# Preparing three more head pairs with VectorE transposes, and taking the mask constant from exp's bias

## The chip, the cores and the metric

The kernel runs on one core of a Trainium2 chip. The metric is the time of one execution in microseconds (us), measured on the device; a lower number is better. Before the change the median was 326.76 us of three runs (325.74 to 328.09). Repeated runs of one kernel spread by 1 to 1.5%, so a difference of 0.3% between two single runs says nothing. A run more than 1.5% above the fastest of its kernel counts as slow and is left out of the ratios. "The profile" and "the trace" are records of one profiled execution of each kernel. Its span is about 2 us shorter than the device time.

## The reference, cut to what matters

There are 4 batches of 8 heads, 768 positions, 64 dimensions a head, and 16 cluster centroids a head. A query sees only the keys of its own cluster. The result goes through a hidden layer with sin.

```python
q_assign = argmax(einsum('bhsd,hcd->bhsc', q_n, c_n), -1)     # k_assign likewise
mask     = q_assign[:, :, :, None] == k_assign[:, :, None, :]
scores   = where(mask, q @ k.T / sqrt(D), -1e9)
attn     = exp(scores - max(scores)); attn = attn / (sum(attn) + 1e-9)
x        = attn @ v                                           # heads side by side, 512 wide
h        = x @ w_in;  g = h + sin(alpha * h)**2 / (alpha + 1e-9)
out      = g @ w_out
```

## The kernel before

Heads are handled two at a time. There are 16 such pairs, m = 0 to 15, four in a batch. A pair takes 12 steps, so a batch takes 48. One step multiplies one block of scores into one of two buffers of PSUM (`scores`), takes its exp (`expo`, 128x768), and multiplies an older exp with v (`pv`). After each batch comes a hidden stage (w_in, sin, w_out), whose rest fills the steps of the next batch.

The mask is put into the matmul. Each query and key carries, besides its 64 dimensions, 16 rows that are 1 in the row of its cluster, and one row more, the sign row: +1 for queries, -1 for keys. The product of these 17 rows is 0 where the clusters agree and -1 where they don't. The exp's scale is 32, so a masked score is multiplied by exp(-32).

```python
KR = D + NHC + 1                       # 64 + 16 + the sign row
NPE = 2 * NHP                          # pairs 0 to 7 are prepared by TensorE
trp = ctx.enter_context(tc.tile_pool(name="trp", bufs=2))
...
def expo(i):
    pT = ptp.tile([P, S], BF16, tag="pT", name="pT")
    nc.scalar.activation(out=pT, in_=area(i)[:, 0:S], func=ACTF.Exp, scale=escale)
```

Before a pair's scores can start, its q and k are loaded (`load_qk`), transposed so that the 64 dimensions lie on partitions (tile `T32`), copied into the bf16 operand tile `QK` by GpSimd (`prep_cast`), multiplied with the centroids (`prep_asn`, the cluster product), turned into one-hot rows in four pieces by VectorE (`prep_hot`), and these rows are moved into `QK` by four small DMAs (`prep_move`). There are two ways of transposing:

```python
def prep_T(m, g, bk=None, eng="dve"):  # TensorE: three fp32 transposes, then one copy
    for jj in range(NJ2):
        nc.tensor.transpose(out=bk[:, P*jj : P*jj+P], in_=src[:, h, P*jj : P*jj+P], identity=ident_f)
    nc.vector.tensor_scalar_mul(out=s["T32"][:, g, :], in0=bk[:, 0:HS], scalar1=1.0 / QDIV)
...
def prep_D(m, g):                      # VectorE: 32x32 blocks are transposed in place ...
    nc.vector.transpose(out=s["Tq"][:, g, :], in_=src[:, h, :].rearrange("p (j e d) -> p e j d", e=2, d=32))
def prep_S(m):                         # ... and 8 DMAs carry the blocks to their partitions
    s["T32"] = trp.tile([P, 4, HS], F32, tag="T32", name="T32")
    for i in range(4):
        for e in range(2):
            lo = D * (i // 2) + 32 * e
            nc.sync.dma_start(out=s["T32"][lo : lo+32, :, ...], in_=s["Tq"][32*i : 32*i+32, :, ...])
...
first = {1: 0, 2: 4, 3: 12, 4: 20, 5: 28, 6: 36}     # the step at which a pair's preparation starts
# prep(m, s0), for m >= NPE: prep_D at s0-5.., prep_S at s0-2; then s0 += 12;
# prep_cast at s0+2 and s0+4; prep_asn at s0+5: 19 steps from the DMAs to their reader
...
# w_in and w_out: four loads at steps 23, 30, 36, 42 of batch 0, four at step 47
```

The way by VectorE spares TensorE, but it puts DMAs between the load and the cluster product, and these need time to land. The kernel before uses it from pair 8 on.

The softmax here doesn't subtract the row's maximum and nothing guards it: scores larger than these inputs give would overflow.

## Time and profile before

| stage (us) | before |
|---|---|
| head: start to first exp | 14.09 |
| batch 0: first exp to the first sin table | 44.43 |
| hidden stage 0 | 29.85 |
| batch 1, 2, 3 | 43.47, 43.75, 41.57 |
| hidden stages 1, 2 | 29.68, 29.45 |
| tail: from the last sin table | 48.71 |
| span | 325.0 |

The stages are cut at ScalarE's table loads: a stage of attention is the time from an exp table to the next sin table. In the page of the profile of before, the lines below are: busy time of each engine, the clock that TensorE was granted and the DMA engines' busy share (each digit is tenths, in one of 40 slices), the share of each engine in the chain that ended last, two groups of instructions (busy time, mean ns of one, idle time before them), and one group of DMAs (KB each, us from issue to landing).

```profile
span 325.0 us, 7163 instructions
PE 306.9 (94%) x2744; PEld 183.3 (56%) x2787; DVE 206.1 (63%) x361; ACT 241.7 (74%) x325; POOL 112.6 (35%) x175
...
PEclk9989999999999999999999999999999999999999
DMA  7455398993016959550043858520043200000031
...
PE 70%; ACT 10%; DVE 9%; issue 5%; POOL 3%; DMA 2%; SPq 1%; ACTq 0%; DVEq 0%; POOLq 0%
...
L319 ACT ACTIVATE pT<-S 128x768 bf16<-128x768 f32 x192 | 145.3, 810 | 27.1 <-PE S L314 24.8
...
L400 ACT ACTIVATE s_sb<-S,alpha_col 128x768 bf16<-128x768 f32 x44 | 39.4, 902 | 24.2 <-PE S L389 14.2
...
T<-Tq SPq DMA_DIRECT2D x64, 96.0 KB, 3.4
```

TensorE is busy for 94% of the span, its clock is full nearly everywhere, and DMA is 2% of the chain. Two groups of ScalarE deserve a second look: the exp and the sin have the same shape and the same source in PSUM, but the exp, with immediate scale, takes 810 ns, and the sin, whose scale is a tile of one value a partition (`alpha_col`), takes 902 ns.

The next view is the table of windows for batch 0 (busy us of each engine with its count, then the clock, the DMA engines' busy share, and GB/s).

```profile
core 0: us, PE busy (x) PEld busy (x) DVE busy (x) ACT busy (x) POOL busy (x), PEclk, DMA share, GB/s
14.00:62.00 48.00, 45.20 (x537) 30.50 (x536) 35.22 (x67) 38.40 (x49) 37.46 (x49) 0.96 0.69 171
...
19.50:58.30 38.80, 36.05 (x452) 24.84 (x452) 30.67 (x59) 32.72 (x43) 31.66 (x41) 1.00 0.66 168
```

From 19.5 to 58.3 TensorE is busy 36.05 of 38.80 us and ScalarE 32.72. The timeline of ScalarE: its columns are start, duration, engine, line, operation, count of instructions in a row without a gap, and in brackets the idle time before, with its releaser.

```profile
14.09 1.51 ACT L319 ACTIVATE pT<-S 128x768 bf16<-128x768 f32 x2 [3.03 <-PE S L314]
...
46.48 4.70 ACT L319 ACTIVATE pT<-S 128x768 bf16<-128x768 f32 x6 [0.64 <-PE S L314]
...
261.52 9.16 ACT L319 ACTIVATE pT<-S 128x768 bf16<-128x768 f32 x12 [0.25 <-PE S L314]
```

Every gap shown is ended by a score matmul of TensorE.

### The profile page before, as it was taken

The numbers are of one execution on the slowest core, as the hardware profiler recorded it, in microseconds if no ns is written. First come the engines' busy times: TensorE is split into PE (matmuls) and PEld (weight loads), VectorE is DVE, ScalarE is ACT, GpSimd is POOL, SyncE is SP. The second block draws the span as 40 slices with busy tenths as digits, with TensorE's granted clock in tenths as the row PEclk, the third lists the DMA queues.
The fourth block names the chain that finished last, engine by engine and source line by source line (L and its number), as shares of the span: only waits on it lengthen the run. The fifth ranks groups of instructions, "written<-read, shape, count | busy, mean of one in ns | idle before, by whom it ended". The sixth has DMA issues, their size and how long they took to land.

```text
span 325.0 us, 7163 instructions
## 1 busy us (share of the span) xinstructions
PE 306.9 (94%) x2744; PEld 183.3 (56%) x2787; DVE 206.1 (63%) x361; ACT 241.7 (74%) x325; POOL 112.6 (35%) x175
## 2 busy tenths in 40 slices
PE   6699999899999999999999999999999999999995
PEld 3276666555555665555556565555556566555544
DVE  4468888387837566677837766677836522577721
ACT  5388888787778988787678888787778999687300
POOL 7848797620017089530005476430006200000000
PEclk9989999999999999999999999999999999999999
DMA  7455398993016959550043858520043200000031
GB/s 228 139 189 162 123 217 187 216 206 118 2 65 198 242 129 248 199 177 2 0 125 97 235 114 245 130 81 2 0 114 96 61 35 34 0 35 0 0 126 70
DMA packets 26290, 37.78 MB, mean 116 GB/s; under 512 B 3880, under 2 KB 20112, under 8 KB 26256
## 3 DMA queue, kind: packets, MB, share of 16 engines
q0 software_dynamic: 8704, 19.93, 23.8%
q1 hardware_dynamic: 17312, 17.33, 19.3%
q8 instruction: 22, 0.36, 0.5%
q14 instruction: 12, 0.10, 0.1%
q10 hardware_dynamic: 240, 0.06, 0.1%
HBM read 27.30 MB, written 6.29 MB: 103 GB/s over the span
## 4 chain that ended last, share of the span: by engine, by line
PE 70%; ACT 10%; DVE 9%; issue 5%; POOL 3%; DMA 2%; SPq 1%; ACTq 0%; DVEq 0%; POOLq 0%
PE S L389 17%; PE M L360 13%; PE S L313 9%; ACT pT L319 8%; PE M L389 8%; PE OB L328 6%; PE OB L360 4%; PE S L314 4%; PE M L211 3%; PE S L360 2%; POOL QK L185 1%; SPq L175 1%; DVE Tq L164 1%; PE M L352 1%; PE M L143 1%
## 5 line engine op out<-in xcount | busy, mean ns | idle before, releaser
L319 ACT ACTIVATE pT<-S 128x768 bf16<-128x768 f32 x192 | 145.3, 810 | 27.1 <-PE S L314 24.8
L360 PE MATMUL M<-w_out_bf,gT 128*128 128x512 bf16 (+1 forms) x259 | 82.1, 372 | 0.6 <-DVE asT L243 0.3
L313 PE MATMUL S<-QK 81*128 81x512 bf16 x192 | 73.7, 384 | 6.5 <-DMA QK<-ohT 2.3
L389 PEld LDWEIGHTS <-w_in_bf 128*128 128x128 bf16 x512 | 49.6, 98 | 39.0 <-issue 3.1
L328 PEld LDWEIGHTS <-pT 128*128 128x128 bf16 x1152 | 56.0, 98 | 24.2 <-DVE xs L340 3.0
L389 PE MATMUL S<-xT,w_in_bf 128*128 128x512 bf16 (+1 forms) x348 | 65.0, 325 | 1.4 <-DVE gT L409 0.8
L190 POOL TENSOR_SCALAR QK<-T 64x384 bf16<-64x384 f32 x64 | 33.3, 520 | 92.5 <-DMA T<-Tq 78.6
L328 PE MATMUL OB<-VX,pT 128*128 128x65 bf16 x1152 | 61.2, 194 | 1.4 <-DVE xs L340 1.4
L400 ACT ACTIVATE s_sb<-S,alpha_col 128x768 bf16<-128x768 f32 x44 | 39.4, 902 | 24.2 <-PE S L389 14.2
L360 PEld LDWEIGHTS <-gT 128*128 128x128 bf16 x400 | 39.0, 98 | 27.2 <-issue 1.0
L314 PE MATMUL S<-QK 81*128 81x256 bf16 x192 | 52.4, 273 | 0.0
L409 DVE SCALAR_TENSOR_TENSOR gT<-u_sb,ralpha,S 128x768 bf16<-128x768 bf16 x44 | 44.5, 1013 | 11.4 <-ACT u_sb L405 8.1
L185 POOL CAST QK<-T 64x768 bf16<-64x768 f32 x32 | 26.6, 830 | 45.1 <-DVE T L149 39.1
L314 PEld LDWEIGHTS <-QK 81*128 81x128 bf16 x192 | 18.9, 99 | 22.2 <-issue 7.7
L389 PE MATMUL M<-xT,w_in_bf 128*128 128x512 bf16 (+1 forms) x156 | 29.7, 324 | 0.7 <-DVE gT L409 0.5
L407 DVE TENSOR_TENSOR u_sb<-s_sb 128x768 bf16<-128x768 bf16 x40 | 23.1, 577 | 7.8 <-ACT s_sb L400 7.8
L339 DVE RECIPROCAL rec<-OB 128x6 f32<-128x6 f32 x32 | 6.0, 187 | 34.4 <-PE OB L328 34.4
L313 PEld LDWEIGHTS <-QK 81*128 81x128 bf16 x192 | 18.8, 98 | 15.0 <-issue 10.8
L409 DVE SCALAR_TENSOR_TENSOR gT<-u_sb,ralpha,M 128x512 bf16<-128x512 bf16 (+1 forms) x40 | 22.8, 611 | 6.4 <-ACT u_sb L405 6.0
L400 ACT ACTIVATE s_sb<-M,alpha_col 128x512 bf16<-128x512 f32 (+1 forms) x40 | 20.9, 574 | 7.4 <-PE M L389 7.4
L360 PE MATMUL OB<-w_out_bf,gT 128*128 128x512 bf16 (+1 forms) x76 | 24.6, 357 | 0.0
L405 ACT ACTIVATE u_sb<-s_sb 128x768 bf16<-128x768 bf16 x24 | 20.2, 843 | 0.8
(82 smaller groups left out, 261.6 us busy)
## 6 DMA issues: line engine op xcount, KB each, us to landing
T<-Tq SPq DMA_DIRECT2D x64, 96.0 KB, 3.4
out_dram<-o_sb SPq DMA_DIRECT2D x23, 256.0 KB, 2.1
v<-in_v_dram POOLq DMA_DIRECT2D x14, 384.0 KB, 4.5
q<-in_q_dram POOLq DMA_DIRECT2D x13, 384.0 KB, 5.1
k<-in_k_dram POOLq DMA_DIRECT2D x13, 384.0 KB, 6.2
w_in_bf<-in_moe_w_in_dram POOLq DMA_DIRECT2D x4, 512.0 KB, 8.0
w_out_bf<-in_moe_w_out_dram POOLq DMA_DIRECT2D x4, 512.0 KB, 11.1
QK<-ohT SPq DMA_DIRECT2D x60, 24.0 KB, 4.3
```

The lines of the kernel that those rows point to most:

```text
L185: nc.gpsimd.tensor_copy(out=QK[0:D, m % NQK, h, :, HS * par : HS * par + HS], in_=src)
L190: nc.gpsimd.tensor_scalar(out=QK[0:D, m % NQK, h, t].rearrange("c (n i a) -> c i n a", i=4, a=32)[:, 2 * par : 2 * par + 2], in0=src[:, t] ...
L313: nc.tensor.matmul(out=dst[:, 0:512], lhsT=lhsT, rhs=T[:, 0, 0:512], start=True, stop=True)
L314: nc.tensor.matmul(out=dst[:, 512:S], lhsT=lhsT, rhs=T[:, 0, 512:S], start=True, stop=True)
L319: nc.scalar.activation(out=pT, in_=area(i)[:, 0:S], func=ACTF.Exp, scale=escale)
L328: nc.tensor.matmul(out=o3[:, j, :], lhsT=pT[:, P * j : P * j + P], rhs=VX[m % NVX][:, h, jof(m // NHP, kt), :], start=(kt == 0 and j == 0) ...
L360: nc.tensor.matmul(out=bk[:, lo:hi], lhsT=gT[:, f, P * mt : P * mt + P], rhs=w_out_bf[:, f, lo:hi], start=(f == 0), stop=(f == NF - 1),)
L389: nc.tensor.matmul(out=ar[lo // 512][:, 0 : hi - lo] if isinstance(ar, tuple) else ar[:, lo:hi], lhsT=lhsT, rhs=xT[:, kk, lo:hi], start=(k ...
L400: nc.scalar.activation(out=s_sb[:, lo:hi], in_=src, func=ACTF.Sin, scale=alpha_col[:, f : f + 1])
L405: nc.scalar.activation(out=u_sb, in_=s_sb, func=ACTF.Square)
L407: nc.vector.tensor_tensor(out=u_sb, in0=s_sb, in1=s_sb, op=ALU.mult)
L409: nc.vector.scalar_tensor_tensor(out=gT[:, f, lo:hi], in0=u_sb[:, lo:hi], scalar=ralpha[:, f : f + 1], in1=src, op0=ALU.mult, op1=ALU.add,)
```

## The change

It was meant to take work off TensorE and off the head. Pairs 4 to 6 go by VectorE instead of TensorE (12 groups of three transposes fewer on TensorE in batch 0). Weights are loaded from step 1 on, so that the hidden stage never waits for them. The sign row goes, and its -1 becomes a bias of -32 in the exp. In the head, v and pair 2 are loaded behind the moves of pair 0's one-hot rows, and the sum of squares of the centroids is made by one Square with a sum on ScalarE. Cluster products are split in halves over two steps, to fit between score blocks.

```diff
-    NPE = 2 * NHP
+    NPE = NHP
+    MIX = NHP + 3            # pair 7: still by TensorE, but in the later batches' order of positions
-    trp = ... bufs=2
+    trp = ... bufs=3
-    KR = D + NHC + 1
+    KR = D + NHC
@@ expo
-    nc.scalar.activation(out=pT, in_=area(i)[:, 0:S], func=ACTF.Exp, scale=escale)
+    nc.scalar.activation(out=pT, in_=area(i)[:, 0:S], func=ACTF.Exp, scale=escale, bias=nbias)
@@ head
+    nbias = const.tile([P, 1], F32, name="nbias");  nc.vector.memset(nbias, -escale)
-    sgn = ...  (tile, memsets, and two DMAs into QK)
     load_qk(1)
-    load_v(0)
-    load_qk(2)
-    nc.vector.tensor_tensor(out=csq, in0=c_sb, in1=c_sb, op=ALU.mult)
-    nc.vector.tensor_reduce(out=cnrm, in_=csq, axis=AXX, op=ALU.add)
+    nc.scalar.activation(out=csq, in_=c_sb, func=ACTF.Square, accum_out=cnrm)
     nc.scalar.activation(out=cnrm, in_=cnrm, func=ACTF.Sqrt)
@@
     head_move(0, 0, [nc.sync, nc.scalar])
+    load_v(0)
+    load_qk(2)
@@ the plan: pair: (steps of the transposes), (steps of the casts), step of the cluster product, way
+        4: ((10, 11, 16, 17), (30, 31), 32, prep_D),
+        5: ((21, 22, 24, 25), (38, 39), 40, prep_D),
+        6: ((33, 34, 36, 37), (49, 50), 51, prep_D),
+        7: ((), (52, 54), 56, prep_T),
+        8: ((48, 49, 50, 52), (65, 66), 68, prep_D),
+    for m in range(9, NP):
+        k0 = STEPS * (m - 3)
+        plan_of[m] = ((k0-12, k0-11, k0-9, k0-8), (k0 + 5, k0 + 6), k0 + 8, prep_D)
+    # the first half of a cluster product one step earlier; prep_S at the fourth transpose
@@ weights
-    steps 23, 30, 36, 42, 47, 47, 47, 47
+    steps  1,  9, 19, 27, 35, 40, 44, 47
... (earlier loads of q, k and v, those of pairs 8 to 10 held back to hidden stage 0; the cnB copy with head 0 first;
...  pair 7's order of positions; the fillers' steps)
```

More of the change, by code (lines that the diff above doesn't have):

```diff
@@ L57 @@
     vldp = ctx.enter_context(tc.tile_pool(name="vldp", bufs=2))
-    trp = ctx.enter_context(tc.tile_pool(name="trp", bufs=2))
+    trp = ctx.enter_context(tc.tile_pool(name="trp", bufs=3))
     tqp = ctx.enter_context(tc.tile_pool(name="tqp", bufs=2))
@@ L188, in prep_cast @@
                 continue
+            if m == MIX:
+                nc.gpsimd.tensor_copy(
+                    out=QK[0:D, m % NQK, h].rearrange("c t (jj e p) -> e c t jj p", e=2, p=P)[par],
+                    in_=src.rearrange("c t (jj p) -> c t jj p", p=P),
+                )
+                continue
             for t in range(2):
@@ L202, in prep_v, with prep_asn @@
         nc.gpsimd.tensor_copy(out=VX[m % NVX][:, :, :, 0:D], in_=st[m]["v32"])
-    def prep_asn(m, bk=None):
+    def prep_asn(m, part=0, parts=1):
         s = st[m]
         hp = pair_of[m][1]
-        bk = bank() if bk is None else bk
+        if part == 0:
+            s["asn"] = bank()[:, 0:HS]
+        w = HS // parts
         for g in range(4):
             nc.tensor.matmul(
-                out=bk[32 * g : 32 * g + 32, 0:HS],
+                out=s["asn"][32 * g : 32 * g + 32, w * part : w * part + w],
                 lhsT=cnB[:, 2 * hp + g // 2, :],
-                rhs=s["T32"][:, g, :],
+                rhs=s["T32"][:, g, w * part : w * part + w],
                 start=True,
@@ L217, in prep_asn @@
             )
-        s["asn"] = bk[:, 0:HS]
     def head_asn(m, h, bk):
@@ L265, in prep_hot @@
             s["ohT"] = smp.tile([P, 2, HS], BF16, tag="ohT", name="ohT")
-            if m >= NPE:
+            if m == MIX:
+                nc.vector.transpose(
+                    out=s["ohT"].rearrange("p a n -> p (a n)"),
+                    in_=s["oh"].rearrange("p par (jj i) c -> p jj par (i c)", i=4),
+                )
+            elif m >= NPE:
                 nc.vector.transpose(
@@ L443 @@
     nc.vector.memset(warm, 0.0)
+    nbias = const.tile([P, 1], F32, name="nbias")
+    nc.vector.memset(nbias, -escale)
     cnB = const.tile([P, H, 2 * NHC], F32, name="cnB")
@@ L451 @@
         nc.gpsimd.memset(oh, 0.0)
-    sgn = const.tile([1, 2, S], BF16, name="sgn")
-    for t in range(2):
-        nc.gpsimd.memset(sgn[:, t, :], 1.0 if t == 0 else -1.0)
     for i in range(NVX):
@@ L457 @@
     load_qk(1)
-    load_v(0)
-    load_qk(2)
     nc.sync.dma_start(out=a_sb, in_=moe_alpha.rearrange("(f p) -> f p", p=P))
-    for t in range(2):
-        nc.sync.dma_start(
-            out=QK[D + NHC : KR, :, :, t, :].rearrange("c s h n -> c (s h) n"),
-            in_=sgn[:, t, :].unsqueeze(1).to_broadcast([1, 2 * NQK, S]),
-        )
     def warmup(n):
@@ L478 @@
     csq = const.tile([P, D], F32, name="csq")
-    nc.vector.tensor_tensor(out=csq, in0=c_sb, in1=c_sb, op=ALU.mult)
     cnrm = const.tile([P, 1], F32, name="cnrm")
-    nc.vector.tensor_reduce(out=cnrm, in_=csq, axis=AXX, op=ALU.add)
+    nc.scalar.activation(out=csq, in_=c_sb, func=ACTF.Square, accum_out=cnrm)
     nc.scalar.activation(out=cnrm, in_=cnrm, func=ACTF.Sqrt)
     nc.vector.tensor_scalar_add(out=cnrm, in0=cnrm, scalar1=1e-6)
-    crn = const.tile([P, 1], F32, name="crn")
-    nc.vector.reciprocal(out=crn, in_=cnrm)
     cn_dup = const.tile([P, 2, D], F32, name="cn_dup")
+    nc.vector.reciprocal(out=cnrm, in_=cnrm)
     nc.vector.tensor_scalar_mul(
-        out=cn_dup, in0=c_sb.unsqueeze(1).to_broadcast([P, 2, D]), scalar1=crn[:, 0:1]
+        out=cn_dup, in0=c_sb.unsqueeze(1).to_broadcast([P, 2, D]), scalar1=cnrm[:, 0:1]
     )
@@ L492 @@
     nc.tensor.transpose(out=OB[:, 0:P], in_=cn_dup, identity=ident_f)
-    for par in range(2):
-        rows = slice(D * par, D * par + D)
-        nc.vector.tensor_copy(
-            out=cnB[rows, :, NHC * par : NHC * par + NHC],
-            in_=OB[rows, 0:P].rearrange("p (h c) -> p h c", c=NHC),
-        )
+    for h0, h1 in ((0, 1), (1, H)):
+        for par in range(2):
+            rows = slice(D * par, D * par + D)
+            nc.vector.tensor_copy(
+                out=cnB[rows, h0:h1, NHC * par : NHC * par + NHC],
+                in_=OB[rows, NHC * h0 : NHC * h1].rearrange("p (h c) -> p h c", c=NHC),
+            )
     etab = const.tile([P, 1], F32, name="etab")
-    nc.scalar.activation(out=etab, in_=crn, func=ACTF.Exp)
+    nc.scalar.activation(out=etab, in_=cnrm, func=ACTF.Exp)
     head_asn(0, 0, M0)
@@ L529, in at @@
         plan.setdefault(i, []).append(fn)
-    def prep(m, s0):
-        if m == 1:
-            s0 -= 4
-        else:
-            for g in range(4):
-                if m < NPE:
-                    if m != NHP + 3 or g == 3:
-                        at(s0 + g, lambda g=g: prep_T(m, g))
-                else:
-                    at(s0 - 5 + g, lambda g=g: prep_D(m, g))
-            if m >= NPE:
-                at(s0 - 2, lambda: prep_S(m))
-                s0 += STEPS
-            at(s0 + 2, lambda: prep_cast(m, 0))
-            at(s0 + 4, lambda: prep_cast(m, 1))
-        at(s0 + 5, lambda: (prep_asn(m), prep_hot(m, 0)))
-        at(s0 + 6, lambda: (prep_hot(m, 1), prep_hot(m, 2)))
-        at(s0 + 7, lambda: (prep_hot(m, 3), prep_move(m)))
@@ L550, with hot_steps @@
-    first = {1: 0, 2: 4, 3: 12, 4: 20, 5: 28, 6: 36}
-    for b in range(1, B):
-        for n in range(NHP):
-            if NHP * b + 3 + n < NP:
-                first[NHP * b + 3 + n] = ASTEPS * b + 2 + STEPS * n
-    for m, s0 in first.items():
-        prep(m, s0)
-        if m == NHP + 3:
-            at(ASTEPS - 8, lambda m=m: load_qk(m, eng=nc.gpsimd))
-        elif m > 2:
-            at(max(0, s0 - 14), lambda m=m: load_qk(m, eng=nc.gpsimd))
+    asn_at = set()
+    def hot_steps(m, a):
+        asn_at.add(a)
+        if 1 < a < ASTEPS:
+            at(a - 1, lambda: prep_asn(m, 0, 2))
+            at(a, lambda: (prep_asn(m, 1, 2), prep_hot(m, 0)))
+        else:
+            at(a, lambda: (prep_asn(m), prep_hot(m, 0)))
+        at(a + 1, lambda: prep_hot(m, 1))
+        at(a + 2, lambda: prep_hot(m, 2))
+        at(a + 3, lambda: (prep_hot(m, 3), prep_move(m)))
@@ new lines, in pair_steps @@
+    def pair_steps(m, make, cast, a, src):
+        if m > 1:
+            for g, i in enumerate(make):
+                at(i, lambda g=g: src(m, g))
+            if src is prep_D:
+                at(make[3], lambda: prep_S(m))
+            for h in range(2):
+                at(cast[h], lambda h=h: prep_cast(m, h))
+        hot_steps(m, a)
+    plan_of = {
+        1: ((), (), 1, prep_T),
+        2: ((6, 7, 8, 9), (8, 10), 12, prep_T),
+        3: ((14, 15, 16, 17), (16, 18), 20, prep_T),
+        4: ((10, 11, 16, 17), (30, 31), 32, prep_D),
[3 more added lines that the diff above has]
+        8: ((48, 49, 50, 52), (65, 66), 68, prep_D),
+    }
@@ L561 @@
+    for m in range(9, NP):
+        k0 = STEPS * (m - 3)
+        plan_of[m] = (tuple(k0 + d for d in (-12, -11, -9, -8)), (k0 + 5, k0 + 6), k0 + 8, prep_D)
+    for m, steps in plan_of.items():
+        pair_steps(m, *steps)
+    for m, i in {3: 0, 4: 0, 5: 10, 6: 18, 7: 26, 11: 56, 12: 66, 13: 95, 14: 95, 15: 95}.items():
+        at(i, lambda m=m: load_qk(m, eng=nc.gpsimd))
+    late = [8, 9, 10]
+    pacer = const.tile([1, 1], BF16, name="pacer")
     for m in range(1, NP):
         if m > 1:
-            at(max(0, STEPS * m - 14), lambda m=m: load_v(m, nc.gpsimd))
+            at({2: 2, 3: 12, 4: 24, 5: 36}.get(m, STEPS * m - 26), lambda m=m: load_v(m, nc.gpsimd))
@@ L574, in alpha @@
         nc.vector.reciprocal(out=ralpha, in_=ralpha)
-    at(15, alpha)
+    at(5, alpha)
     def load_w_in(n):
@@ L589 @@
     for i, fn, n in (
-        (23, load_w_in, 0),
-        (30, load_w_out, 0),
-        (36, load_w_in, 1),
-        (42, load_w_in, 2),
-        (ASTEPS - 1, load_w_out, 1),
-        (ASTEPS - 1, load_w_in, 3),
-        (ASTEPS - 1, load_w_out, 2),
+        (1, load_w_in, 0),
+        (9, load_w_out, 0),
+        (19, load_w_in, 1),
+        (27, load_w_in, 2),
+        (35, load_w_out, 1),
+        (40, load_w_in, 3),
+        (44, load_w_out, 2),
         (ASTEPS - 1, load_w_out, 3),
@@ L618 @@
                 fn()
-            if fill and r % STEPS != 7:
+            if fill and i not in asn_at:
                 fill.go(1)
@@ L637 @@
                 fill.go(10 if f == 2 else 64, "act")
-            if b == 0 and f < 3:
-                prep_T(NHP + 3, f, (M0, OB, M0)[f], "act")
+            if b == 0 and f < 4:
+                prep_T(NHP + 3, f, (M0, OB, M0, M0)[f], "act")
+            if b == 0 and f == 8:
+                nc.gpsimd.tensor_copy(out=pacer, in_=gT[0:1, f - 2, 0:1])
+                for m in late:
+                    load_qk(m, eng=nc.gpsimd)
             for mt, bk, lag in own:
```

## The prediction

> **What bounds it now.** Span 325.0 us, clock 0.995. By the table of windows: a head (first exp at 14.09 in the timeline), batch 0's attention to 58.5, then hidden-layer stages of about 33 us alternating with attention stages of 39.4, 40.0 and 37.5 us, and a tail. Batches 1 to 3 and the hidden stages are bound by TensorE (busy 37.8 of 39.4, 38.7 of 40.0, 33.2 of 33.5). Batch 0 is near a tie: 48 exps of 0.81 us are 38.9 us of ScalarE, but it lasts 44.4; the 5.5 us are waits for score matmuls (0.4 to 0.9 us each), which fall where TensorE also does fp32 transposes (three take about 0.26 us) or a pair's cluster product (0.78 us).
>
> **What changes.**
> 1. Head. The sign row and its two DMAs (which held the SP queue from 6.28 to 9.6) go; v and pair 2 move behind pair 0's one-hot moves. Now the first scores start at 13.56, released by such a move, whose SP half was issued only at 9.98. Against it: the order of instructions shows an extra table load between Square and Sqrt. A load takes 1283 ns in this trace, as the Trainium skill states (ScalarE: Activation LUTs, "What ACT_TABLE_LOAD costs"). It puts pair 0's copies about 0.9 us later and the centroids about 1.1, in spite of the split cnB copy and two VectorE operations saved. I estimate moves issued at 9.9, first scores at 12.5: 1.0 us gained. v then lands about 15, so the first PV product and pair 1's casts (behind v's cast) wait: up to 1 us given back.
> 2. Batch 0. 12 groups of TensorE transposes leave (about 3.1 us), pair 6's cluster product moves to batch 1 (0.78), the others are halved and so fit the slack of two score buffers. TensorE falls below ScalarE. VectorE exchanges copies of 0.55 for transposes of 0.53 us. Estimate: waits 5.5 to about 3 us.
> 3. Added DMA in batch 0: three pairs' moves (8 x 96 KB each) and four more weight loads. The DMA share is already 0.9 to 1.0 in 40 to 64; I expect saturation from about 25 us on, moves landing in 4 to 8 us instead of 3.4, and some TensorE wait at pair 4's or 5's cluster product (steps 31, 39). Cost 0.5 to 1.5 us.
> 4. Exp with a bias tile: still 0.81 us. 80 rows instead of 81: nothing.
> 5. Hidden stage 0 did not wait for weights, so earlier weights gain nothing there. Batch 1 gets two more cluster products (+1.6), minus a transpose group and a filler; batch 3 one less (-0.8). Net about +0.3 us.
>
> **Critical path.** Head -1.0, batch 0 -2.5, DMA waits and late v together +1, later stages +0.3: about -2.2. The tuned step numbers suggest that the DMA waits are smaller than I fear, so I take -3.3.
>
> **Prediction.** 323.4 us, 8 in 10 between 319.8 and 327.0. Faster by over 2% 0.11, within 2% 0.86, slower by over 2% 0.03.
>
> **What would show it.** First exp at 12.5 to 13.5 (step 1); ScalarE busy above 90% in batch 0, hidden stage starting at 55 to 56.5 (2); DMA share near 1.0 from 25 to 60 and TensorE waits released by DMA (3); exp mean 810 ns (4); batch 1 longer by about 1 us, batch 3 shorter (5).
>
> **What would make it wrong.** DMA saturation delaying pair 3's load or pair 4's moves by several us (slower); the split cluster product removing nearly all waits of batch 0 (faster by up to 6 us); the head gaining nothing because of the table load.

## The result, and the profile after

The change made the kernel slower: 342.95 us median of four runs (339.63 to 344.55), beside 326.79 of before. The ratio is 1.048, with a 95% interval of 1.039 to 1.057. Ratios here are the mean time of one kernel's fast runs over the mean of the other's fast runs of the same rounds, so they are not quite the ratio of the medians. The output was correct.

The page of the profile of after, with the lines that answer to those of before:

```profile
span 340.3 us, 7214 instructions
PE 313.8 (92%) x2741; PEld 183.3 (54%) x2783; DVE 204.8 (60%) x361; ACT 257.2 (76%) x329; POOL 114.4 (34%) x186
...
PEclk9997995999999999999999999999999999999999
DMA  6479999980716596780007756620011000000022
...
PE 57%; ACT 21%; DMA 7%; DVE 6%; issue 5%; POOL 1%; SPq 1%; DVEq 0%; ACTq 0%; POOLq 0%
...
L332 ACT ACTIVATE pT<-S,nbias 128x768 bf16<-128x768 f32 x192 | 158.8, 903 | 27.6 <-PE S L327 26.2
...
T<-Tq SPq DMA_DIRECT2D x88, 96.0 KB, 4.6
```

Three things changed on this page. The exp takes 903 ns instead of 810. The DMA engines are full through batch 0, and DMA rose from 2% to 7% of the chain. And TensorE, with about as many instructions, is busy longer (313.8 against 306.9 us), while its clock drops in two places, to tenths 7 and 5 (what that cost is estimated below). The stage table puts the loss into the head and batches 0 and 1, with a small part in batches 2 and 3:

| kernel | span | head | batch 0 | hidden 0 | batch 1 | hidden 1 | batch 2 | hidden 2 | batch 3 | tail |
|---|---|---|---|---|---|---|---|---|---|---|
| before | 325.0 | 14.09 | 44.43 | 29.85 | 43.47 | 29.68 | 43.75 | 29.45 | 41.57 | 48.71 |
| after | 340.3 | 15.25 | 51.30 | 30.07 | 48.82 | 29.59 | 44.32 | 29.51 | 43.11 | 48.33 |

The span grew by 15.3 us: 1.2 in the head, 6.9 in batch 0, 5.3 in batch 1, 0.6 in batch 2, 1.5 in batch 3; the other stages differ by less than 0.4. This is one profiled run of each kernel, and that of before is a little slow in batch 0: its TensorE ran at half clock from 14.88 to 18.30 while it was busy, which b_bias0, after and a_pe456_nobias_sq below did not. An estimate of what that is worth is half of it, 1.7 us.

ScalarE's timeline of after shows the head's new table load, batch 0 with its gaps, and an undisturbed run of batch 3:

```profile
3.93 1.28 ACT L486 ACT_TABLE_LOAD   x1
...
15.25 10.80 ACT L332 ACTIVATE pT<-S,nbias 128x768 bf16<-128x768 f32 x13 [2.80 <-PE S L327]
...
49.47 1.69 ACT L332 ACTIVATE pT<-S,nbias 128x768 bf16<-128x768 f32 x2 [2.56 <-PE S L327]
...
266.39 9.75 ACT L332 ACTIVATE pT<-S,nbias 128x768 bf16<-128x768 f32 x12 [0.16 <-PE S L327]
```

Two exps in a row now take 1.69 us instead of 1.51. Batch 0 starts well, with 13 exps in a row; later ScalarE stops several times, for 2.56 us before the exps at 49.47. It is TensorE that came late there. TensorE's timeline of after has its own waits:

```profile
28.96 0.54 PE L341 MATMUL OB<-VX,pT 128*128 128x65 bf16 x12 [1.29 <-DVE xs L353]
...
48.41 0.53 PE L220 MATMUL M<-T,cnB 128*32 128x192 f32 x8 [2.49 <-issue]
...
56.98 0.86 PE L220 MATMUL M<-T,cnB 128*32 128x192 f32 x8 [1.31 <-DMA QK<-ohT]
...
130.16 0.85 PE L220 MATMUL M<-T,cnB 128*32 128x384 f32 x8 [2.48 <-DMA out_dram<-o_sb]
```

L220 is the cluster product, which reads the moved tile `T`. The releasers in the brackets are guesses of the profile and don't name that tile. GpSimd's timeline does: its cast of the same tile starts at the same moment, and names the move. The last of the eight moves had been issued at 39.65 and landed at 48.32, 8.7 us later.

```profile
48.49 3.56 POOL L197 TENSOR_SCALAR QK<-T 64x384 bf16<-64x384 f32 x6 [5.01 <-DMA T<-Tq]
```

The wait at 28.96 has another source. VectorE had to normalise an output there, but stood in front of it at pair 4's transpose, whose load had not landed:

```profile
26.14 0.58 DVE L165 STREAM_TRANSPOSE Tq<-q 128x384 f32<-128x384 f32 x1 [2.56 <-DMA q<-in_q_dram]
```

The wait at 130.16, in batch 1, is one for a moved tile too: the last of pair 9's moves, issued at 121.96, landed at 129.97.

Now the windows of after: first all engines over batch 0, as before, then TensorE alone in stretches of 2 us, then in stretches of 3.41 us just before half clock set in twice, and around the wait at 130.16.

```profile
14.00:62.00 48.00, 39.42 (x448) 25.21 (x449) 28.96 (x59) 35.58 (x43) 35.85 (x52) 0.86 1.01 248
```
```profile
core 0: us, PE busy (x), PEclk, DMA share, GB/s
28.00:30.00 2.00, 1.04 (x16) 0.89 1.15 299
30.00:32.00 2.00, 2.00 (x17) 0.50 1.22 204
46.00:48.00 2.00, 0.00 (x0) 1.00 1.11 278
50.00:52.00 2.00, 1.88 (x18) 0.51 1.18 232
56.00:58.00 2.00, 1.02 (x9) 0.50 1.23 208
60.00:62.00 2.00, 1.65 (x22) 0.93 1.05 167
...
26.16:29.58 3.42, 1.93 (x27) 1.00 1.19 261
46.64:50.06 3.42, 1.65 (x30) 1.00 1.06 269
125.15:128.57 3.42, 2.54 (x29) 1.00 0.71 162
128.57:131.98 3.41, 1.77 (x23) 1.00 0.69 178
```

In the same 48 us the DMA share is 1.01 instead of 0.69, and TensorE's clock 0.86 instead of 0.96. After the waits at 28.96 and 48.41, TensorE runs at half clock for a while: it is busy in all of 30 to 32 but finishes 17 matmuls there, and the second spell lasts some ten microseconds from 50 on, with the wait at 56.98 inside it. The wait at 130.16, as long as that at 48.41, had no such effect.

The clock records of the traces tell these waits apart. In all 17 traces the clock changes on a grid of 3.41 us, and a spell of half clock in mid-kernel is one, two or three such stretches long (here 29.58 to 32.99, and 50.06 to 60.30). Up to 320 us, every stretch at full clock with TensorE busy for less than 1.7 us was followed by half clock, none with more than 2.5 us was, and between the two both occurred. The wait that ended at 130.16 fell across a boundary of the grid and left 2.54 and 1.77 us busy on its two sides. So whether a wait costs clock too depends on where it falls on the grid, which nobody chose.

An estimate of what half clock cost, from the same view in windows of 4 us: busy time times the missing clock is 4.00 x 0.37 in 30 to 34, 6.49 x 0.5 in 50 to 58 and 3.65 x 0.29 in 58 to 62, together 5.8 us of TensorE time.

### The profile page after: what moved, and what is told of

It is laid out like the page before. It is cut to its first block, busy times and chain, and to the rows that moved or that the text cites. A ratio compares the mean times of both kernels' runs of the same rounds, so it can differ in the third digit from the quotient of the medians.

```text
span 340.3 us, 7214 instructions
## 1 busy us (share of the span) xinstructions
PE 313.8 (92%) x2741; PEld 183.3 (54%) x2783; DVE 204.8 (60%) x361; ACT 257.2 (76%) x329; POOL 114.4 (34%) x186
## 4 chain that ended last, share of the span: by engine, by line
PE 57%; ACT 21%; DMA 7%; DVE 6%; issue 5%; POOL 1%; SPq 1%; DVEq 0%; ACTq 0%; POOLq 0%
ACT pT L332 19%; PE S L402 15%; PE M L373 11%; PE M L402 7%; PE S L326 7%; PE OB L373 4%; PE OB L341 4%; PE M L220 3%; PE S L327 2%; DMA T<-Tq 2%; PE S L373 2%; DVE gT L422 2%; DMA k<-in_k_dram 2%; PE M L365 1%; ACT s_sb L413 1%
## 5 line engine op out<-in xcount | busy, mean ns | idle before, releaser
L332 ACT ACTIVATE pT<-S,nbias 128x768 bf16<-128x768 f32 x192 | 158.8, 903 | 27.6 <-PE S L327 26.2
L326 PE MATMUL S<-QK 80*128 80x512 bf16 x192 | 74.6, 389 | 8.2 <-ACT pT L332 3.6
L341 PEld LDWEIGHTS <-pT 128*128 128x128 bf16 x1152 | 57.4, 99 | 23.6 <-DVE xs L353 1.9
L402 PE MATMUL S<-xT,w_in_bf 128*128 128x256 bf16 (+1 forms) x345 | 64.8, 325 | 1.4 <-DVE gT L422 0.8
L197 POOL TENSOR_SCALAR QK<-T 64x384 bf16<-64x384 f32 x88 | 45.9, 521 | 40.3 <-DMA T<-Tq 30.5
L413 ACT ACTIVATE s_sb<-S,alpha_col 128x768 bf16<-128x768 f32 x44 | 39.3, 900 | 23.5 <-PE S L402 13.4
L327 PE MATMUL S<-QK 80*128 80x256 bf16 x192 | 53.1, 277 | 0.0
L373 PEld LDWEIGHTS <-gT 128*128 128x128 bf16 x400 | 38.9, 97 | 26.2 <-issue 1.3
L327 PEld LDWEIGHTS <-QK 80*128 80x128 bf16 x192 | 18.9, 99 | 29.5 <-issue 21.1
L402 PE MATMUL M<-xT,w_in_bf 128*128 128x256 bf16 (+1 forms) x154 | 29.4, 324 | 0.3
L209 POOL CAST VX<-v 128x768 bf16<-128x768 f32 x16 | 13.4, 840 | 38.4 <-PE OB L341 34.8
L326 PEld LDWEIGHTS <-QK 80*128 80x128 bf16 x192 | 19.0, 99 | 13.0 <-issue 10.7
L118 POOL DMA_DIRECT2D q<-in_q_dram x13 | 9.6, 737 | 40.2 <-DVE Tq L165 40.1
```

The source lines that it names most:

```text
L197: nc.gpsimd.tensor_scalar(out=QK[0:D, m % NQK, h, t].rearrange("c (n i a) -> c i n a", i=4, a=32)[:, 2 * par : 2 * par + 2], in0=src[:, t] ...
L209: nc.gpsimd.tensor_copy(out=VX[m % NVX][:, :, :, 0:D], in_=st[m]["v32"])
L326: nc.tensor.matmul(out=dst[:, 0:512], lhsT=lhsT, rhs=T[:, 0, 0:512], start=True, stop=True)
L327: nc.tensor.matmul(out=dst[:, 512:S], lhsT=lhsT, rhs=T[:, 0, 512:S], start=True, stop=True)
L341: nc.tensor.matmul(out=o3[:, j, :], lhsT=pT[:, P * j : P * j + P], rhs=VX[m % NVX][:, h, jof(m // NHP, kt), :], start=(kt == 0 and j == 0) ...
L373: nc.tensor.matmul(out=bk[:, lo:hi], lhsT=gT[:, f, P * mt : P * mt + P], rhs=w_out_bf[:, f, lo:hi], start=(f == 0), stop=(f == NF - 1),)
```

## The experiments

Two theories stood against each other. Theory A: pairs 4 to 6 by VectorE load the DMA engines and bring the moved tiles late, and TensorE pays in waits and in clock. Theory B: the bias tile makes each exp 93 ns longer, which is 192 x 0.093 = 17.9 us of ScalarE, and so explains the whole loss. Smaller suspects were the early weight loads, the step numbers of the cluster product, and the head. Each edit is against the kernel named; times are medians, and the ratio is to the runs of before in the same rounds.

### 1. b_bias0: the kernel before, with a bias tile of zeros

```diff
-    nc.scalar.activation(..., func=ACTF.Exp, scale=escale)
+    nc.scalar.activation(..., func=ACTF.Exp, scale=escale, bias=zbias)   # zbias = 0.0
```

> The kernel before, with one edit: the exp takes a bias tile of zeros (128x1 in SBUF); everything else, the sign row too, stays. Theory 'bias operand': each exp rises from 811 to about 900 ns and the closest spacing of two exps from about 0.72 to 0.81 us, so that ScalarE's floor for 48 exps rises from 34.4 to 38.9 us and the kernel is 2 to 6 us slower (329 to 333). Rival 'the longer exp comes from something else in the changed kernel' (80 rows, DMA traffic, clock): exps stay at 811 ns and the time stays within 1 us of before.

330.96 us (330.46 to 331.94), ratio 1.011 (1.006 to 1.017). The group of the exp:

```profile
L319 ACT ACTIVATE pT<-S,zbias 128x768 bf16<-128x768 f32 x192 | 158.3, 905 | 17.7 <-PE S L314 16.9
```

The exp becomes 95 ns longer (905 instead of 810 ns) for the tile alone, and the busy time grows by 13.0 us. But ScalarE's idle time before the exps falls from 27.1 to 17.7 us, and only 3.5 us reach the total. Theory B explains a part, not the whole.

### 2. a_nobias: the change without the bias

```diff
-    ... func=ACTF.Exp, scale=escale, bias=nbias)
+    ... func=ACTF.Exp, scale=escale)
```

Without the sign row and without the bias, every score that agrees is 32 higher instead of every other being 32 lower. The division by the sum takes a common factor out, and the result is correct.

> The changed kernel without the bias in the exp, and still without the sign row: a softmax does not change when all its scores shift by one constant, so the result stays right (weights up to e^32 are in range of bf16 and fp32). Theory 'bias operand is the larger half': exps return to 811 ns, time falls from 343 to about 335 (8 us). Theory 'DMA waits are the larger half': exps return to 811 ns but TensorE still waits for the moves of the transposed tiles, time falls by 2 to 4 us only (339 to 341).

340.45 us (339.3 to 341.32), ratio 1.039 (1.034 to 1.044).

```profile
L332 ACT ACTIVATE pT<-S 128x768 bf16<-128x768 f32 x192 | 145.4, 811 | 39.1 <-PE S L327 36.1
```

The exp is back at 811 ns. Busy time fell by 13.4 us, idle time rose by 11.5, and the median by only 2.5 us. A part of the gain was lost to the clock: in batch 1 the wait that ended at 130.16 in after lasts 3.25 us here, half clock follows it (129.00 to 135.82), and batch 1 is 2.0 us longer than in after. Still, something else holds most of the loss.

### 3. a_pe456: the change, with pairs 4 to 6 back on TensorE

```diff
-    NPE = NHP;  MIX = NHP + 3
+    NPE = 2 * NHP;  MIX = -1
-    4: ((10, 11, 16, 17), (30, 31), 32, prep_D), 5: ((21, 22, 24, 25), (38, 39), 40, prep_D), 6: ((33, 34, 36, 37), (49, 50), 51, prep_D)
+    4: ((22, 23, 24, 25), (24, 26), 28, prep_T), 5: ((30, 31, 32, 33), (32, 34), 36, prep_T), 6: ((38, 39, 40, 41), (40, 42), 44, prep_T)
```

With `MIX = -1` pair 7 goes back to the plain order of positions as well, and pair 6's cluster product comes back from batch 1 into batch 0.

> The changed kernel with pairs 4 to 6 transposed by TensorE again (groups at steps 22, 30 and 38 on, as pair 3 has them), nothing else undone. Theory 'DMA waits from the moved tiles': the waits at 26 to 33, 47 to 49 and 55 to 61 us go, batch 0 shortens from 51.3 to about 46 us, and batch 1 is little changed: time 337 to 339. Rival 'the waits come from the earlier weights and late v': batch 0 stays above 50 us, time above 341.

331.54 us (330.58 to 332.67), ratio 1.012 (1.007 to 1.017). This takes away 11.4 of the 16.2 us, although TensorE has its 12 groups of transposes back. Batch 0 takes 43.97 us and batch 1 45.57. The windows of this kernel over batch 0:

```profile
14.00:62.00 48.00, 44.78 (x573) 30.57 (x575) 34.91 (x69) 41.38 (x49) 40.69 (x52) 1.00 0.95 225
```

The clock is 1.00 throughout, although the early weights keep the DMA share at 0.95. TensorE is busier than in after (44.78 against 39.42 us in the same 48), which is what one wants here. Theory A holds the larger part of the loss.

### 4 and 10. a_wlate and a_wnone: later weights

```diff
-    (1, load_w_in, 0), (9, load_w_out, 0), (19, load_w_in, 1), (27, load_w_in, 2), (35, load_w_out, 1), (40, load_w_in, 3), (44, load_w_out, 2)
+    a_wlate: the steps of before: 23, 30, 36, 42, 47, 47, 47
+    a_wnone: all of them at step 47
```

> The changed kernel with the weights loaded at the old steps (23, 30, 36, 42, 47), nothing else undone. Theory 'earlier weights crowd the moves': landing of the moves in batch 0 falls from 8 to about 4 us, the waits at 47 to 49 and 55 to 61 us shrink, time 339 to 341. Rival 'the moves are late for another reason (issue behind VectorE and the SP queue)': time within 1 us of 343.

344.03 us (342.87 to 345.22), ratio 1.050 (1.045 to 1.056): no better than after. That the weights are loaded early is not the cause.

> The changed kernel with all weights loaded at step 47, so that none of them competes in batch 0. Theory 'the moves are slow because the DMA queues are full': the moves of batch 0 land in 3 to 4.5 us instead of 6.4, the waits at pair 4's and 5's cluster product go, batch 0 falls to about 47 us (the wait for pair 4's load stays), while hidden stage 0 grows by some us as it waits for weights. Rival 'the distance of 14 steps is too short even with quiet queues': the waits stay and batch 0 stays above 50 us.

346.31 us (344.25 to 347.24), ratio 1.058 (1.054 to 1.063). Without any weights in batch 0 the moves land in a median of 4.2 us instead of 6.4 (24 moves in the window from 14 to 68; the first line is after's, the second a_wnone's), and batch 0 falls from 51.30 to 48.47 us. But hidden stage 0 grows from 30.07 to 37.40, since its first matmul has to wait for w_in:

```profile
T<-Tq SPq DMA_DIRECT2D x24, 96.0 KB, 6.4
```
```profile
T<-Tq SPq DMA_DIRECT2D x24, 96.0 KB, 4.2
```
```profile
68.13 0.82 PE L402 MATMUL S<-xT,w_in_bf 128*128 128x512 bf16 x2 [5.55 <-DMA w_in_bf<-in_moe_w_in_dram]
```

So traffic matters in batch 0, but the weights have to come at some time, and most of batch 0's loss (48.47 against 43.97 in a_pe456) stays even without them. The run does not show quiet queues, though. The loads of q, k and v still keep the DMA share at 1.05 and 1.06 from 38 to 46, the last of pair 4's moves takes 8.8 us, and TensorE waits 3.03 us for it at 48.16. The wait at pair 5's cluster product is gone.

### 5 and 6. a_asnlate and a_late: more steps between the moves and their reader

```diff
 a_asnlate:
-    4: ((10, 11, 16, 17), (30, 31), 32), 5: ((21, 22, 24, 25), (38, 39), 40)
+    4: ((10, 11, 16, 17), (38, 39), 40), 5: ((21, 22, 24, 25), (44, 45), 46)
 a_late: a_asnlate, and pair 4's transposes behind its load:
+    4: ((16, 17, 18, 19), (38, 39), 40)
```

> The changed kernel, but the casts and the cluster product of pair 4 at steps 38 to 40 (was 30 to 32) and of pair 5 at 44 to 46 (was 38 to 40); both are needed only after hidden stage 0. The moves and transposes stay. Theory 'TensorE waits for the moved tiles and then runs at half clock': the waits at 46 to 48 and 55 to 57 us and the half clock after them go, batch 0 falls from 51.3 to about 46 to 47 us (the stretch at 27 to 33 us stays), time about 338 to 339. Rival 'VectorE's transposes cost by their own work and DMA traffic': batch 0 stays at 50 us or more.

343.02 us (339.69 to 344.19), ratio 1.046 (1.041 to 1.051).

> The kernel of a_asnlate, and pair 4's VectorE transposes at steps 16 to 19 (was 10, 11, 16, 17), when its load has landed. Theory 'VectorE, in order, stood waiting for pair 4's load and TensorE behind it': the 3.1 us that VectorE waited for q and k and the half clock at 29 to 33 us go too, batch 0 falls to about 44 us, as with the transposes back on TensorE, time about 335. Rival 'this wait was hidden': no gain over a_asnlate.

342.02 us (340.35 to 343.52), ratio 1.046 (1.042 to 1.049). Neither moved the total. In a_asnlate the cluster product of pair 4 no longer waits, but the scores behind it do, for the one-hot rows:

```profile
50.76 0.61 PE L326 MATMUL S<-QK 80*128 80x512 bf16 x1 [1.82 <-DMA QK<-ohT]
```

In a_late that wait is 2.59 us at 51.33. A later cluster product means later one-hot rows, and these go through the same queue as the moves. SP's timeline of after shows how close they stand in it (start, and time to issue all of them):

```profile
34.81 5.59 SPq L176 DMA_DIRECT2D T<-Tq  x8
40.50 2.73 SPq L300 DMA_DIRECT2D QK<-ohT  x4
43.40 8.12 SPq L176 DMA_DIRECT2D T<-Tq  x8
```

In after the four rows issued from 40.50 on land from 48.88 on, right behind the last move at 48.32. That they land late because of the moves ahead of them is argued from this order; no run isolates it. What is shown is that a shift of the steps only shifted the wait. VectorE's wait for pair 4's load is not the main matter either: a_late cuts TensorE's wait behind it from 1.7 us in a_asnlate to 0.3, and the time stays (a wait of 1.3 us for GpSimd's copy of v, at 36.62, came in its place).

### 9 and 13. a_relead and a_relead2: more distance for all pairs, 19 steps in the later batches

```diff
 a_relead:
+    4: ((19, 21, 22, 24), (40, 41), 42), 5: ((26, 27, 28, 30), (46, 47), 48), 6: ((34, 35, 37, 38), (56, 58), 60)
+    8: cluster product at 71;  9 and later: casts at k0 + 8, k0 + 9, cluster product at k0 + 11 (19 steps)
 a_relead2: the same, but 5: ((26, 27, 28, 30), (44, 45), 46), and
-    tqp = ... bufs=2
+    tqp = ... bufs=3
```

> The changed kernel with the VectorE transposes kept, but with the old distance from the moves to their first use (18 steps or hidden stage 0 in between, instead of 14 for pairs 4 to 6; 19 instead of 16 for pairs 8 on), and with the moves of pairs 4 and 5 issued just behind pair 3's one-hot moves (step 24) instead of just ahead of them. Theory 'the moves come too late for their first use, and one-hot moves queue behind them': TensorE's waits of 1.3 to 2.8 us and the half clock after them go, batch 0 falls from 51.3 to 44 to 46 us and batch 1 from 48.8 to about 45.5, time 331 to 335. Rival 'with this DMA traffic no order of the steps helps': new waits appear elsewhere, time stays above 338.

349.17 us, and the result was wrong (relative error 0.073), which was not intended. Both have a likely reason in the plan. The steps with a cluster product skip a filler; with six of these in batch 1 the last fillers of batch 0's output came out after the hidden stage had begun to overwrite their operand `gT`. TensorE's timeline shows the wait this made:

```profile
153.02 4.35 PE L373 MATMUL M<-w_out_bf,gT 128*128 128x512 bf16 x10 [4.72 <-DVE gT L422]
```

And with two buffers for `Tq` VectorE stood at its next transpose until the earlier moves had read the buffer:

```profile
54.34 0.58 DVE L165 STREAM_TRANSPOSE Tq<-q 128x384 f32<-128x384 f32 x1 [8.62 <-DMA T<-Tq]
```

Its time settles nothing. The mended version has no more than five of these steps in batch 1 and three buffers; it mends both at once, so which of the two made the result wrong was not tested. Its distances are 18, 16 and 22 steps for pairs 4 to 6, and 19 from pair 8 on:

> a_relead mended: a third buffer for the transposed tiles, so that VectorE need not wait until pair 4's moves have read theirs, and pair 5's cluster product at steps 45 and 46, so that the fillers of batch 1 are as many as in the changed kernel and product 50 no longer reads gT after hidden step 2 has overwritten it (that made a_relead wrong). Theory 'too late for their first use': batch 0 falls from 51.3 to 44 to 46.5 us and batch 1 from 48.8 to 45 to 46, time 331 to 335. Rival 'with this DMA traffic no order of the steps helps': TensorE waits elsewhere, batch 0 stays above 49, time above 338.

338.64 us (337.91 to 339.19), ratio 1.037 (1.033 to 1.040), correct. Batch 1 falls from 48.82 to 45.29 us, and the wait of 2.48 us at 130.16 shown above is gone. So the shorter distance was needed for this loss. It was not enough for it: a_pe456 has the same 16 steps in batch 1 and 45.57 us, and there the last of pair 9's moves lands at 120.20, just before their cluster product at 120.50. The short distance left no margin. In after SP has one more group of one-hot rows to issue in batch 1 (pair 6's) and comes to pair 9's moves only 10.3 us before TensorE wants them, against 12.6 in a_pe456; that this made the difference is argued. Batch 0 falls only from 51.30 to 49.56. Its moves land in 8.0 us now, and it still waits for a moved tile and still falls to half clock:

```profile
59.95 0.87 PE L220 MATMUL M<-T,cnB 128*32 128x192 f32 x8 [2.24 <-DMA T<-Tq]
```
```profile
38.00:42.00 4.00, 3.94 (x31) 0.51 1.15 232
```

### 14. a_pe456_extra: the traffic without its reader

Pairs 4 to 6 are prepared by TensorE as in a_pe456. Besides, VectorE transposes them too, as in the change, and SP moves the blocks into a tile that nobody reads. The expectation below speaks of "the same steps", but in the code they are those of a_pe456 (22 to 25, 30 to 33, 38 to 41) and not those of the change, and there VectorE also copies TensorE's transposes. The moves come later, and pair 6's are issued only from 62.05 on, behind most of batch 0.

```diff
 (against a_pe456)
+    extra = const.tile([P, 4, HS], F32, name="extra")
+    if m in (4, 5, 6):
+        for g, i in enumerate(make): at(i, lambda g=g: prep_D(m, g))
+        at(make[3], lambda: extra_S(m))      # prep_S with extra in T32's place
```

> a_pe456 (331.5 us) with the work of the other path added and its result unused: VectorE transposes pairs 4 to 6 once more at the same steps and the SP queue moves 24 x 96 KB into a scratch tile that nobody reads. Theory 'TensorE loses time because it waits for the moved tiles': the same traffic without a reader costs 0 to 2.5 us (batch 0 44 to 46.5, time 332 to 334). Rival 'the traffic itself and VectorE's work cost': batch 0 rises to 49 us or more, time above 337.

335.58 us (334.72 to 336.02), ratio 1.027 (1.023 to 1.030). Batch 0 takes 48.46 us, 4.5 more than in a_pe456; the other stages stay. The windows over batch 0:

```profile
14.00:62.00 48.00, 42.13 (x531) 28.16 (x532) 37.24 (x77) 38.49 (x46) 38.27 (x50) 1.00 1.02 242
```

The DMA share is 1.02, as in after, but the clock stays at 1.00. So this much traffic and VectorE's work cost time (4.5 us in batch 0) without any reader of the moved tiles and without a drop of the clock. How the 7.3 us that the change lost in batch 0 against a_pe456 divide between them and the waits for moved tiles is not shown: here VectorE does both ways' work at the same steps, which can make the 4.5 too large, and a third of the moves come too late to count, which can make it too small. VectorE had a wait of 1.16 us for the extra moves, and TensorE one of 1.65 us for VectorE. How much of the 4.5 is traffic and how much VectorE stays open too: this kernel was not run with lighter traffic.

### 15 and 7. a_sq and b_nosign: the head

```diff
 a_sq (against after):
-    nc.scalar.activation(out=csq, in_=c_sb, func=ACTF.Square, accum_out=cnrm)
+    nc.vector.tensor_tensor(out=csq, in0=c_sb, in1=c_sb, op=ALU.mult)
+    nc.vector.tensor_reduce(out=cnrm, in_=csq, axis=AXX, op=ALU.add)
 b_nosign (against before):
-    KR = D + NHC + 1
+    KR = D + NHC                             # and no sgn tile, no memsets, no DMAs, no bias
```

> The changed kernel with only the centroids' square back on VectorE, so that one table load between Square and Sqrt goes. Theory: first exp falls from 15.2 to about 14.0, and the time by about as much if nothing later absorbs it (342); since batch 0 then waits for data that do not come earlier, it may be nothing (343).

341.95 us (341.25 to 343.79), ratio 1.048 (1.043 to 1.052). The first exp comes at 13.80 instead of 15.25, but the total is that of after: batches 0 and 1 together took 100.87 us in the profile instead of 100.12. So a head that started 1.45 us earlier gained nothing here; batch 0 still waits for DMAs.

> The kernel before without the sign row and its two DMAs and without any bias (the shift cancels in the softmax). Theory: the SP queue is free 3.3 us earlier, pair 0's moves issue at about 8.8 instead of 9.98, first exp about 1 us earlier (13.1), exps stay at 811 ns; time 325 to 326.5, ratio 0.995 to 0.999. Rival 'v and pair 2 ahead of the moves hold them': first exp unchanged at 14.1.

326.48 us (325.47 to 326.79), ratio 0.998 (0.996 to 1.000). The first exp comes at 13.29 instead of 14.09, in one profiled run of each; the three kernels of the next part differ by 1.6 us in this number, so it is rough. The estimate for the total is a gain of 0.2%, and its interval reaches from 0.4% to nothing.

### 8, 12 and 11. The parts that help: a_pe456_nobias_sq, best_whole, best_vfirst

The first has the three undone parts together: pairs 4 to 6 on TensorE, no bias, Square on VectorE. The sign row stays away. The second makes the cluster products whole again. The third loads v and pair 2 early, as before.

```diff
 a_pe456_nobias_sq = after + edit of a_pe456 + edit of a_nobias + edit of a_sq
 best_whole  (against it):  if 1 < a < ASTEPS:   ->   if False:
 best_vfirst (against it):  load_v(0); load_qk(2) behind load_qk(1) again
```

> The changed kernel with pairs 4 to 6 back on TensorE, no bias and no sign row, and the centroids' square back on VectorE. If the three causes add up (transposes on VectorE -11, bias -3.5, extra table load -1.2), it takes 342.95 - 15.7 = about 327, first exp at about 13; if the remaining parts of the change (early weights, halved cluster products, v behind the moves) are worth something, it falls below the kernel before (below 326); if they cost, it stays above 328.

324.27 us (323.11 to 326.06, six runs), ratio 0.992 (0.989 to 0.995): faster than both kernels, by less than 1% against before. Batch 0 takes 42.72 us instead of 44.43 and batch 2 42.77 instead of 43.75; batch 1 takes 44.33, a little more. A part of this is the clock and not the code. The 36 runs of before in the rounds of the experiments fall into two groups: 15 had a mean clock of 0.998 or more and a median of 326.3 us, 21 a lower clock and 327.5. The six runs here all had 0.998 or more, so at an equal clock about 2 us are left, and the 1.7 us of batch 0 are as much as the half clock in the profiled run of before was worth.

> The kernel of a_pe456_nobias_sq with the cluster products of batch 0 whole again instead of in two halves. If the halves fit the slack of two score buffers, as predicted: batch 0 rises from 42.7 to 43.5 to 44.5 us, time about 325.5. If halving is worth nothing: within 0.3 us of 324.3.

325.01 us (322.74 to 327.87, six runs; 324.57 for the five fast ones), ratio 0.993 (0.989 to 0.997). Halving the cluster products is worth nothing that can be seen.

> The kernel of a_pe456_nobias_sq (324.3 us), with v and pair 2 loaded ahead of pair 0's moves again, as in the kernel before. If 'v behind the moves' was of no use: first exp falls from 14.1 to about 13.3 as in b_nosign, the waits for pair 0's and 1's data stay out, time 323 to 324. If it was of use: first exp later than 14.1 and time above 324.5.

327.64 us (324.11 to 329.97, six runs, two of them slow; about 325.9 for the four fast ones), ratio 0.997 (0.992 to 1.002). It is too uncertain to tell from either. Which of the remaining parts of the change gives what is left of the 0.8% is not isolated.

The stages of the profiled runs, side by side:

| kernel | head | batch 0 | hidden 0 | batch 1 | batch 2 | batch 3 |
|---|---|---|---|---|---|---|
| before | 14.09 | 44.43 | 29.85 | 43.47 | 43.75 | 41.57 |
| b_bias0 | 14.49 | 43.84 | 29.75 | 44.61 | 45.06 | 43.52 |
| after | 15.25 | 51.30 | 30.07 | 48.82 | 44.32 | 43.11 |
| a_nobias | 15.30 | 51.18 | 30.13 | 50.80 | 42.56 | 41.31 |
| a_pe456 | 15.22 | 43.97 | 30.08 | 45.57 | 44.25 | 43.14 |
| a_pe456_extra | 15.29 | 48.46 | 30.08 | 45.44 | 44.25 | 43.13 |
| a_relead2 | 14.90 | 49.56 | 30.86 | 45.29 | 44.75 | 43.00 |
| a_pe456_nobias_sq | 14.11 | 42.72 | 30.13 | 44.33 | 42.77 | 41.14 |

The bias shows best where nothing else waits: in batches 2 and 3 of after and a_nobias it costs 1.8 us each. In batches 0 and 1 of the same two kernels removing it gains nothing, since ScalarE waits there anyway and the clock fell in batch 1 of a_nobias. From a_pe456 to a_pe456_nobias_sq, where those waits are gone, the median falls by 7.3 us (6.6 by the ratios, since the two ran in different rounds); the head's 1.1 us is in that. The costs of the two causes do not add: each hides a part of the other.

## Why the prediction was wrong, point by point

The prediction was 323.4 us, with 319.8 to 327.0 as its range and a chance of 0.03 for slower by over 2%. It was 342.95. The direction was wrong, and the following steps failed.

**Step 3, "Cost 0.5 to 1.5 us", is the main one.** The mechanism was right as it stood: the DMA share went to 1.01, the moves of batch 0 landed in 6.4 us ("4 to 8 us" was said), and TensorE waited at the cluster products of pairs 4 and 5. The size was off by nearly a factor of ten: undoing pairs 4 to 6 gave back 11.4 us, net of what the lighter TensorE was to save. The prediction counted one or two waits of TensorE. It left out that saturated DMA and VectorE's added work cost time before any late tile is waited for (4.5 us in batch 0 of a_pe456_extra, at other steps); that half clock can follow a wait, as it did twice here (an estimate of 5.8 us of TensorE time, part of it hidden); and that the shortened distance leaves batch 1 without margin as well, which lost 3.3 us more than a_pe456 and got it back with 19 steps (a_relead2). How the 11.4 us divide among these stays open.

**Step 4, "Exp with a bias tile: still 0.81 us", was false.** It takes 903 ns. The trace of before had the answer: a sin of the same shape with a scale tile took 902 ns beside the exp's 810. The page "ScalarE: Activation LUTs" of the Trainium skill, section "What ACT_TABLE_LOAD costs", which the prediction cites for the table load, says there too that each pointer operand adds about 93 ns. Alone, on before, the bias costs 3.5 us; in after 2.5; with the DMA waits gone, most of 7.3.

**Step 2, "Batch 0 is near a tie: 48 exps of 0.81 us are 38.9 us of ScalarE", mis-sized the floor.** The same section of the skill says that activations in a row overlap by about 93 ns, and the trace agrees: two in a row took 1.51 us, so 48 need about 47 x 0.70 + 0.81 = 33.7 us, or 35.0 with the usual 0.73. Batch 0 was bound by TensorE in before, with several us of ScalarE to spare. That spare time hid a good part of the bias in b_bias0. With the bias the same sum is 47 x 0.79 + 0.90 = 38.0 us. Both are estimates from two exps in a row. The expected fall of "5.5 to about 3 us" did not come in after; a_pe456_nobias_sq saved 1.7 us in this batch against before, about what the clock explains.

**Step 1, "1.0 us gained" in the head, had the wrong sign.** The first exp came 1.16 us later, at 15.25. The extra table load was seen and costed (1283 ns were said, 1.28 us measured, at 3.93), but it delays the head by more than was set against it: a_sq without it has the first exp at 13.80, and all ten kernels with it have theirs between 14.58 and 15.31. The removed sign row by itself gained 0.8 us in the head in one run (b_nosign). For the total this step is worth nothing, as a_sq shows.

**Step 5 was right for the hidden stages.** They stayed within 0.3 us, and earlier weights gained nothing there. "Batch 1 longer by about 1 us" was too little: it grew by 5.3 us, of which 3.5 went with the longer distance (a_relead2 has 45.29, 1.8 more than before, and the bias alone makes 1.1 in b_bias0). "Batch 3 shorter" was wrong because of the bias: 43.11 us with it, 41.31 in a_nobias.

**The last move, from -2.2 to -3.3 us with the words "The tuned step numbers suggest that the DMA waits are smaller than I fear", had no reading behind it.** The fear itself, "DMA saturation delaying pair 3's load or pair 4's moves by several us", is what happened. A number in somebody's plan is no measurement, and where the one thing that could make a prediction badly wrong is named, its chance belongs into the range and into the 0.03.

## What to carry to other kernels

Taking work off the busiest engine pays only if what replaces it arrives in time: before moving a transpose to another engine plus DMAs, compare the steps between the DMA and its reader with the landing time under the load that the change itself makes, and allow for a missed landing to cost twice, as the wait and as the clock after it. In these traces the clock fell when TensorE was busy for less than about half of a stretch of 3.41 us. Read the cost of an operand form from another instruction of the same trace before calling it free, and take the cost of one instruction from how close two in a row stand, not from its duration. An additive constant before a softmax needs no instruction at all as long as the exps stay in range: dropping both the sign row and the bias was correct for these inputs, and it belongs to the only version that beat the kernel before.

## What the Trainium skill lacked or had wrong

- "TensorE: Matmul & The Clock Gate", section "What's actually happening", gives half clock "after ≥1 idle window (~3.4µs)". The length is right: the traces show a grid of 3.41 us. But a whole idle window was not needed. In after half clock (0.50) followed windows with TensorE busy for 1.93 and 1.65 of 3.41 us (26.16 to 29.58 and 46.64 to 50.06), while windows with 1.77 us busy (128.57 to 131.98, and 53.62 to 57.04 in a_pe456_extra) left the clock at 1.00.
- The same table lets full clock return after about 3.4 us of sustained work. Every return here did follow a window with TensorE busy for at least 86%, but one such window was not always enough: in a_relead2 TensorE was busy for 3.40 of 3.41 us from 38.11 to 41.52, and the clock stayed at 0.50 until 44.94.
- "ScalarE: Activation LUTs", section "What ACT_TABLE_LOAD costs", was right: a bias tile took the exp from 810 to 903 and 905 ns, two in a row overlapped by about 0.1 us, and a table load took 1.28 us. Its drain of 1.38 us beside the load was not seen as a gap of its own: in before the work ahead of the load at 5.49 ends at 5.47, and the work behind it starts at 6.78, as the load ends.
- No page that was read says how long a 96 KB move inside the chip takes under a saturated set of DMA engines: a median of 3.4 us to landing over the whole of before, 6.4 in batch 0 of after, 8.0 in batch 0 of a_relead2.
